# Where the first expert's weight splits, a route and six norms stand between the attention stage and the expert stages

## The chip, the cores and the metric

The kernel runs on one core of one Trainium2 chip. The metric is device time in microseconds, the median of the runs shown; one more execution was taken with the hardware profiler, and all rows of traces come from it. TensorE, VectorE, ScalarE, GpSimd (POOL) and the DMA queues each work through an instruction list of their own, in the order in which the program's scheduler put them, and wait for each other by semaphores. In the rows PE is TensorE's matmul, DVE is VectorE, ACT is ScalarE, SPq is the queue of SyncE, from which most transfers are issued.

## The reference, cut to what is computed

```python
kv  = einsum('bhsd,bhse->bhde', k, v)          # 4 x 8 heads, 576 rows, 64 columns
out = einsum('bhsd,bhde->bhse', q, kv)
x   = out / sqrt(mean(out*out, -1) + 1e-6) * g_norm      # -> 2304 rows of 512

# stage 1: one expert of 8 for each row
xn, en = x / (norm(x) + 1e-6), emb / (norm(emb) + 1e-6)
logits = xn @ en.T / tau
e      = argmax(logits);  gate = max(softmax(logits))
y      = gate * (relu(x @ w1[e]) @ w2[e])                # 512 -> 1024 -> 512

# stage 2: two experts of 8 for each row, noisy logits, weights from a softmax of the two
out    = sum over the two experts of weight * (relu(y @ w1b[e]) @ w2b[e])
```

All data is float32. The argmax of stage 1 needs only the direction of x, so the norm of a row enters the gate, not the choice of expert.

## The kernel before, in words

**Attention.** The 2304 rows lie in 18 tiles of 128 rows, in ten groups (`GROUPS`: two tiles each, but groups 4 and 9, which have one: tiles 8 and 17). For each group k of the loop at L592 the kernel multiplies q by the small matrices `kvm` (`out_mm`, L450; they also hold eight columns that give the logits), squares the results (`rms`, L465 on ScalarE, reduced at L466 on VectorE), takes 1/rms by Ln and Exp on ScalarE (L468, L469), and writes the scaled rows and logits (`out_fin`, L479 to L483, on VectorE). `q_turn` transposes q for the group two ahead (L440, copied on ScalarE at L442). `norms(k)` multiplies a tile by g (L490, VectorE) and sums its squares (L493, ScalarE) into `nx2`, which only the gate reads. It works in the buffers `xq` of the pool `at`; groups 0 to 4 (nine tiles) have their norms in the loop, groups 5 to 9 (nine tiles) behind it.

**Route of stage 1.** `route1(c0, c, psum)` takes the logits of c tiles: maximum, one-hot `hf`/`hb` on VectorE, ranks on TensorE (`ranks`, L200 to L203), slot numbers `si_all`, then c scatters on POOL (L211) that write the rows to `xs_dram`, sorted by expert. `FIRST` calls it in the loop for tiles 0 to 5, 6 to 10 and 11; it is called for tiles 12 to 17 behind the loop. Unit A is the first 256 rows of expert 0: its room is filled from tiles 0 to 11, so its rows are read back (`rows_of`, `xgA`) while attention still runs.

**Weights.** Each float32 weight is split into two fp32r parts, hi = round(w) on ScalarE (L256) and lo = w − hi on VectorE (L258), and a product is three matmuls (hi·hi, lo·hi, hi·lo). `w_load(g)` loads the g-th quarter of an expert's w1 and w2 into two staging buffers, `w_split(g, part)` splits one of them into a ring of four (`RING`; the first two, `PRE`, lie in `ring0`, the others in `ring1`, whose memory is that of the pool `at`). `W_AT` says behind which groups of attention g = 0 and 1 are split: 8 and 9. The names `st_377` and `st_381` are the staging buffers of g = 0 and 1.

**The seam.** Behind the loop stand, in the program: the route of the last six tiles (L622), the transposes of unit A's rows and their split into `xhA`/`xlA` (`x_parts`, L316 on ScalarE, L318 on VectorE; the transposes of the second half take the PSUM buffer `kvp`, which the route's ranks use too), four dummy products that keep TensorE at work (L635), and nine norms behind `xlA`. Then the pools `at` and `ap` close and the pools of the expert stages open on their memory: `mo` (SBUF) and `pp` (PSUM, tags `w` with three buffers and `acc` with five). `last_route` (L736) then counts rows (`slots_end`, L909, a small matmul that reads `cbb`), makes slots for padding rows, computes the gates (`gate1`) and writes them to memory.

**Expert stages.** `run` goes through units of rows and, for each, eight steps f of 128 of the 1024 inner columns: `mm1(u, f)` is 12 matmuls (L753), evicted as `hh` on ScalarE (L755) and `hl` on VectorE (L756); `mm2(u, f)` 12 more (L777) from `hh`, `hl`. So unit A is 8 × 24 = 192 matmuls of 256 columns. `hh`/`hl` have two buffers. Unit B is 128 more rows of expert 0; it needs its rows (`xgA` again) and, at its end, its gates (`ga1B`, gathered by POOL). Then come experts 1 to 7, and stage 2 in the same way. Between steps `weights_to` issues the next splits and loads. The zero-fill of `out` is transferred from a tile that a memset at L672 clears (tag `ot`, three buffers).

Of the kernel before, what the change touches and what calls it, by code (L numbers as in the profile page):

```python
# [8 lines left out]
F32 = mybir.dt.float32  # L9
# [7 lines left out]
P = 128  # L17
B, H, S, D = 4, 8, 576, 64
NT, DM, FF, E = B * S, H * D, 1024, 8
KD, KF = DM // P, FF // P  # L20
RB = S // D
# [11 lines left out]
XW = DM + E + 1  # L33
# [18 lines left out]
def attention_moe_moe_kernel(ctx: ExitStack, tc: tile.TileContext, q, k, v, g_norm, emb, tau, w1a, w2a,  # L52
# [293 lines left out]
    with tc.tile_pool(name="at", bufs=1) as at, \  # L346
# [9 lines left out]

        emb_t = at.tile([E, DM], F32, name="emb_t", tag="xq", bufs=2)
        G.dma_start(emb_t, emb)
# [125 lines left out]

        def norms(k):

            g, r, m = GROUPS[k]
            for c in range(g * RB + r, g * RB + r + m):
                xg = at.tile([P, H, D], F32, name="xq", bufs=2)
                V.tensor_tensor(xg, row_tile[c][:, 0:DM].rearrange("p (h d) -> p h d", d=D),  # L490
                                g_b.unsqueeze(1).to_broadcast([P, H, D]), op=OP.mult)
                xg = xg.rearrange("p h d -> p (h d)")
                A.activation(xg, xg, AF.Square, accum_out=nx2[:, c:c + 1])  # L493
# [98 lines left out]
        for k in range(last + 1):  # L592
            out_mm(k)
            if k == 1:
                for j in range(KD):
                    kv_part(1, j)
                kv_out(1)
                row_block(8, at.tile([P, 8, XW], F32, name="rows1", tag="ld", bufs=5), 4)
            if k in (2, 3):
                kv_m(k)  # L600
            rms(k)
            if k + 2 <= last:
                q_turn(k + 2)
            out_fin(k)
            if 1 <= k <= EARLY_N:
                norms(k - 1)
            if k in FIRST:
                with tc.high_priority():
                    for _ in route1(*FIRST[k], kvp):
                        pass  # L610
                    if k == 6:
                        more_room(cnt1, eoff1)
            if k == 6:
                masks(u1[0:1], u1[0].cnt)
                early.append(rows_of(u1[0]))
            if k in W_AT:
                g = W_AT.index(k)
                w_split(g, 0, V)
                w_split(g, 1, V)
        rooted = pin[0]  # L620
        pin[:] = None, None
        with tc.high_priority():  # L622
            for _ in route1(12, 6, kvp):
                pass
        u = u1[0]
        x = xs[u] = (c_tile([P, KD, A1], F32R, "xhA"), c_tile([P, KD, A1], F32R, "xlA"))
        for c in range(A1N):
            ps = ap.tile([P, 4, P], F32, name="kvp" if c else "qtp")
            for d in range(KD):
                turned = TE.transpose(ps[:, d, :], u.g[:, c, d * P:(d + 1) * P], ident)  # L630
            parted = x_parts(u, x, c, ps, rooted, add_counts.last)
        with tc.issue_after(turned.ins):
            ps = ap.tile([P, 2, 512], F32, name="op", bufs=3)
            for _ in range(4):
                TE.matmul(ps[:, 0, :], lhsT=ones, rhs=ones.unsqueeze(1).to_broadcast([P, 4, P]), start=True, stop=True)  # L635
        with tc.issue_after(parted[0].ins), tc.issue_after(parted[1].ins):
            for k in range(EARLY_N, last + 1):
                norms(k)
        G.dma_start(wgn[:, :, 0:E], w_gate.rearrange("(k p) e -> p k e", p=P))
# [6 lines left out]
        blank = spare[:, 0, :]  # L646
        w_load(PRE)
        w_load(PRE + 1)

# [86 lines left out]
    def last_route():  # L736
        with tc.high_priority():
            rest_of_firsts()
            gate1(0, TC)
            gates_out()  # L740

# [304 lines left out]
    def run(units, post):  # L1046
# [3 lines left out]
        for k, (u, f) in enumerate(steps):  # L1050
# [3 lines left out]
            if rows:  # L1054
# [4 lines left out]
                continue  # L1059
            if first:  # L1060
                if u.name == "A" and u.kind == 1:
                    last_route()
                mm1(u, f)
                first = False
# [257 lines left out]

W_AT = (8, 9)
EARLY_N = 5
WARM = 16
# [26 lines left out]
```

## Time and profile before

| | |
|---|---|
| median of 3 runs | 922.8 us (917.74 to 923.0) |
| profiled execution | 919.37 us, span 917.6 us |
| busy TensorE, VectorE, ScalarE, POOL | 90%, 52%, 35%, 32% of the span |
| mean granted TensorE clock | 0.955 of full speed |
| DMA | 133.7 MB, mean 146 GB/s |
| attention to the first product of unit A | 0 to 128.9 us |
| unit A | 128.9 to 154.2 us |

The profile is read by stretches: the busy shares over the whole span are a mean over stages with different limits. In rows of the timeline a line gives the start in us, how long, the engine, the line of the program, the output and input tile, shapes, and in brackets how long the engine stood idle before it and what released it. [...]

### The profile page before, as it was taken

How to read it: one execution, taken by the hardware profiler on the slowest of the kernel's cores; microseconds unless marked ns; L12 is line 12 of the kernel's file. 1: busy time of each engine (PE TensorE's matmuls, PEld its weight loads, DVE VectorE, ACT ScalarE, POOL GpSimd, SP SyncE). 2: the span in 40 equal slices, each digit the busy share in tenths (PEclk: the TensorE clock that was granted, in tenths of full speed). 3: DMA queues.
4: the chain of work that ended last, by engine and by line, in shares of the span. 5: the costliest groups of instructions: out<-in, count | busy, mean ns of one | idle time of the engine just before them, and what ended most of it. 6: DMA issues, size and time to landing. Idle time of an engine off the chain costs nothing. (4 is left out here: it accounts for less than half of the span.)

```text
span 917.6 us, 15847 instructions
## 1 busy us (share of the span) xinstructions
PE 827.8 (90%) x6190; PEld 753.9 (82%) x6190; DVE 481.6 (52%) x1370; ACT 323.7 (35%) x551; POOL 290.0 (32%) x299
## 2 busy tenths in 40 slices
PE   2778359999999999999969999999999999999993
PEld 1666249899999999998859998988989989899893
DVE  1248884688877967978435344333433333334211
ACT  0045452545435435434124233332323333332210
POOL 5002245428448457143352105023050140300303
PEclk7699669999999999999989999999999999999997
DMA  8961364837666676474266337355283371720404
GB/s 265 332 159 73 123 203 150 256 121 231 174 218 208 181 228 212 127 231 148 79 156 195 88 97 164 93 132 126 69 187 92 117 150 46 185 83 10 58 1 60
DMA packets 80480, 133.70 MB, mean 146 GB/s; under 512 B 10062, under 2 KB 42926, under 8 KB 79504
## 3 DMA queue, kind: packets, MB, share of 16 engines
q1 hardware_dynamic: 60448, 97.78, 35.1%
q0 software_dynamic: 17312, 28.96, 14.3%
q10 hardware_dynamic: 2640, 5.90, 2.0%
q8 instruction: 50, 0.82, 0.4%
q14 instruction: 30, 0.25, 0.1%
HBM read 97.80 MB, written 49.80 MB: 161 GB/s over the span
## 5 line engine op out<-in xcount | busy, mean ns | idle before, releaser
L753 PE MATMUL w<-xh,w1h 128*128 128x320 f32 (+3 forms) x736 | 236.1, 321 | 2.5 <-ACT xh L316 1.5
L753 PE MATMUL w<-xl,w1h 128*128 128x320 f32 (+3 forms) x736 | 229.6, 312 | 0.2 <-DVE xl L318 0.2
L753 PE MATMUL w<-xh,w1l 128*128 128x320 f32 (+3 forms) x736 | 229.7, 312 | 0.0
L755 ACT ACTIVATE hh<-w 128x320 fp32r<-128x320 f32 (+3 forms) x192 | 83.6, 436 | 229.9 <-PE w L753 207.6
L1011 POOL DMA_INDIRECT out_dram<-ot,to x35 | 55.3, 1581 | 295.9 <-DVE ot L1010 287.2
L756 DVE SCALAR_TENSOR_TENSOR hl<-w,hh 128x320 fp32r<-128x320 f32 (+3 forms) x192 | 92.8, 487 | 98.7 <-ACT hh L755 98.7
L753 PEld LDWEIGHTS w<-xh,w1h 128*128 128x128 f32 x736 | 139.3, 189 | 4.8 <-ACT xh L316 1.7
L753 PEld LDWEIGHTS w<-xl,w1h 128*128 128x128 f32 x736 | 139.7, 190 | 2.3 <-DVE xl L318 0.4
L753 PEld LDWEIGHTS w<-xh,w1l 128*128 128x128 f32 x736 | 139.2, 189 | 0.0
L779 PE MATMUL acc<-w2h,hl 128*128 128x512 f32 x320 | 126.8, 396 | 5.6 <-DVE hl L756 5.6
L779 PE MATMUL acc<-w2h,hh 128*128 128x512 f32 x320 | 127.4, 398 | 2.9 <-DVE ot L1010 2.8
L779 PE MATMUL acc<-w2l,hh 128*128 128x512 f32 x320 | 125.7, 393 | 0.0
L258 DVE TENSOR_TENSOR w2l<-st,w2h 128x1024 fp32r<-128x1024 f32 x64 | 79.8, 1246 | 79.0 <-ACT w2h L256 78.6
L258 DVE TENSOR_TENSOR w1l<-st,w1h 128x1024 fp32r<-128x1024 f32 x64 | 78.9, 1232 | 52.2 <-ACT w1h L256 51.9
L256 ACT ACTIVATE w2h<-st 128x1024 fp32r<-128x1024 f32 x64 | 67.7, 1058 | 90.9 <-PE acc L779 72.0
L256 ACT ACTIVATE w1h<-st 128x1024 fp32r<-128x1024 f32 x64 | 67.6, 1057 | 42.0 <-PE w L753 38.4
L777 PE MATMUL acc<-hl,w2h 128*128 128x336 f32 (+1 forms) x256 | 80.2, 314 | 0.4 <-DVE hl L756 0.4
L777 PE MATMUL acc<-hh,w2l 128*128 128x336 f32 (+1 forms) x256 | 79.9, 313 | 0.0
L777 PE MATMUL acc<-hh,w2h 128*128 128x336 f32 (+1 forms) x256 | 78.8, 316 | 0.0
L779 PEld LDWEIGHTS acc<-w2h,hl 128*128 128x128 f32 x320 | 60.3, 189 | 20.1 <-DVE hl L756 5.8
L779 PEld LDWEIGHTS acc<-w2h,hh 128*128 128x128 f32 x320 | 60.2, 188 | 16.1 <-DVE ot L1010 5.5
L779 PEld LDWEIGHTS acc<-w2l,hh 128*128 128x128 f32 x320 | 60.2, 188 | 10.7
(326 smaller groups left out, 1143.4 us busy)
## 6 DMA issues: line engine op xcount, KB each, us to landing
st<-in_moe_w_dram SPq DMA_DIRECT2D x128, 512.0 KB, 4.2
xg<-ys_dram SPq DMA_DIRECT2D x7, 1302.5 KB, 6.6
out_dram<-ot SPq DMA_DIRECT2D x7, 768.0 KB, 5.9
xg<-xs_dram SPq DMA_DIRECT2D x7, 683.8 KB, 5.5
q<-in_q_dram SPq DMA_DIRECT2D x3, 1152.0 KB, 19.7
k<-in_k_dram SPq DMA_DIRECT2D x2, 1152.0 KB, 20.5
k<-in_k_dram ACTq DMA_DIRECT2D x2, 1152.0 KB, 15.3
v<-in_v_dram SPq DMA_DIRECT2D x2, 1152.0 KB, 25.7
```

Source lines behind the costliest of these rows:

```text
L256: A.activation(hi, src, AF.Copy)
L258: eng.tensor_sub(lo, src, hi)
L753: last = TE.matmul(ps, lhsT=w[a][:, d, fo:fo + P], rhs=x[b][:, d, c0:c1], start=(d == 0 and i == 0), stop=(d == KD - 1 and i == 2))
L755: ra = A.activation(h[0][:, c0:c1], ps, AF.Relu)
L756: rv = V.scalar_tensor_tensor(h[1][:, c0:c1], ps, 0.0, h[0][:, c0:c1], op0=OP.max, op1=OP.subtract)
L777: TE.matmul(ac[j], lhsT=w_f[a][:, f % 2, j * P:(j + 1) * P], rhs=h_f[b][:, 0:u.m], start=st, stop=sp)
L779: TE.matmul(ac[j], lhsT=h_f[a][:, j * P:(j + 1) * P], rhs=w_f[b][:, f % 2, :], start=st, stop=sp)
L1011: i = G.indirect_dma_start(out=out, out_offset=bass.IndirectOffsetOnAxis(ap=u.to[:, t:t + 1], axis=0), in_=o, in_offset=None, bounds_check ...
```

## The change

Four things are edited.

1. `W_AT` becomes (1, 3): the weights g = 0 and 1 are split behind groups 1 and 3 of attention, and the loads of g = 2 and 3 are issued right behind each of these pairs of splits, where before they stood at the end of the seam.
2. The route of tiles 12 to 17 is no longer called at the seam. `last_route` now calls it, with a PSUM buffer of the expert stage, and `last_route` itself is called behind the first `mm1` of unit A, its instructions given to the scheduler as ones to be issued after that product.
3. `norms` takes a list of tiles, a pool, a name and a number of buffers. Groups 0 to 5 (tiles 0 to 10) and tile 11 have their norms in the loop, in `xq`; tiles 12 to 17 have theirs in `last_route`, between the count of rows and the gates, in the `ot` buffers of the pool `mo`.
4. Unit A's rows are split behind the last group's operations (`rooted` is now both pins: ScalarE's last Exp and VectorE's last logits), where VectorE's half stood behind the last route's counts.

```diff
-        def norms(k):
-            g, r, m = GROUPS[k]
-            for c in range(g * RB + r, g * RB + r + m):
-                xg = at.tile([P, H, D], F32, name="xq", bufs=2)
-                V.tensor_tensor(xg, row_tile[c][:, 0:DM].rearrange("p (h d) -> p h d", d=D),
+        def norms(cs, pool, nm, bufs):
+            for c in cs:
+                xg = pool.tile([P, XW], F32, name=nm, bufs=bufs)[:, 0:DM]
+                V.tensor_tensor(xg.rearrange("p (h d) -> p h d", d=D), row_tile[c][:, 0:DM].rearrange("p (h d) -> p h d", d=D),
                                 g_b.unsqueeze(1).to_broadcast([P, H, D]), op=OP.mult)
...
-            if 1 <= k <= EARLY_N:
-                norms(k - 1)
...
+            if 1 <= k <= 6:
+                norms(tiles(k - 1), at, "xq", 2)
+            elif k == 7:
+                norms((11,), at, "xq", 2)
             if k in W_AT:
                 g = W_AT.index(k)
                 w_split(g, 0, V)
                 w_split(g, 1, V)
-        rooted = pin[0]
+                w_load(PRE + g)
+        rooted = tuple(pin)
         pin[:] = None, None
-        with tc.high_priority():
-            for _ in route1(12, 6, kvp):
-                pass
...
-            parted = x_parts(u, x, c, ps, rooted, add_counts.last)
+            x_parts(u, x, c, ps, *rooted)
...
-        with tc.issue_after(parted[0].ins), tc.issue_after(parted[1].ins):
-            for k in range(EARLY_N, last + 1):
-                norms(k)
...
-        w_load(PRE)
-        w_load(PRE + 1)
...
     def last_route():
         with tc.high_priority():
+            for _ in route1(12, 6, misc):
+                pass
             rest_of_firsts()
-            gate1(0, TC)
-            gates_out()
+        norms(range(12, 18), mo, "ot", 3)
+        gate1(0, TC)
+        gates_out()
...
             if first:
+                m = mm1(u, f)
                 if u.name == "A" and u.kind == 1:
-                    last_route()
-                mm1(u, f)
+                    with tc.issue_after(m.ins):
+                        last_route()
                 first = False
...
-W_AT = (8, 9)
-EARLY_N = 5
+W_AT = (1, 3)
```

Three places show how the order of instructions moves. Line numbers of the changed kernel are up to six lower behind the edit (L753 becomes L749, L755 becomes L751, L777 becomes L773, L493 becomes L491, L909 becomes L905).

On ScalarE, in attention behind the Exp of group 3, before:

```order
L469 ACTIVATE ry<-rt 128x16
L442 COPY qT<-qtp 128x512
L468 ACTIVATE rt<-ss 128x8
L469 ACTIVATE ry<-rt 128x8
L442 COPY qT<-qtp 128x512
```

and now:

```order
L469 ACTIVATE ry<-rt 128x16
L256 ACTIVATE w1h<-st_381 128x1024
L256 ACTIVATE w2h<-st_382 128x1024
L468 ACTIVATE rt<-ss 128x8
L442 COPY qT<-qtp 128x512
L469 ACTIVATE ry<-rt 128x8
L442 COPY qT<-qtp 128x512
```

The pair of splits for g = 1 stands ahead of the copy of a transposed q tile (tile 11) and of group 4's Ln. The pair for g = 0 stands in the same way behind group 1's Exp.

On ScalarE at the seam, from the split of unit A's rows on, before (the staging buffers `st_1595` to `st_1600` hold g = 2 and 3):

```order
L316 ACTIVATE xhA<-qtp,g_99 128x4x128
L316 ACTIVATE xhA<-kvp,g_99 128x4x128
L493 ACTIVATE xq,nx_197<-xq 128x512 x9
L256 ACTIVATE w1h<-st_1595 128x1024
L176 ACTIVATE rtn<-nx_197 128x18
L256 ACTIVATE w2h<-st_1596 128x1024
L177 ACTIVATE ryn<-rtn 128x18
L256 ACTIVATE w1h<-st_1599 128x1024
L256 ACTIVATE w2h<-st_1600 128x1024
L755 ACTIVATE hh<-w 128x256 x8
```

and now (`st_788` to `st_1036` hold g = 2 and 3):

```order
L316 ACTIVATE xhA<-qtp,g_99 128x4x128
L316 ACTIVATE xhA<-kvp,g_99 128x4x128
L256 ACTIVATE w1h<-st_788 128x1024
L256 ACTIVATE w2h<-st_789 128x1024
L256 ACTIVATE w1h<-st_1035 128x1024
L491 ACTIVATE ot,nx_197<-ot 128x512
L751 ACTIVATE hh<-w 128x256
L491 ACTIVATE ot,nx_197<-ot 128x512 x3
L256 ACTIVATE w2h<-st_1036 128x1024
L491 ACTIVATE ot,nx_197<-ot 128x512 x2
L751 ACTIVATE hh<-w 128x256
```

Three splits and one norm stand ahead of the first eviction, five norms and a split between the first and the second.

On TensorE, between the dummy products and the first product of unit A, before:

```order
L635 LDWEIGHTS ones
L635 MATMUL op<-ones 128x512
L909 LDWEIGHTS ones
L909 MATMUL w<-cbb,ones 128x8
L753 MATMUL w<-xhA,w1h 128x256
```

and now, from the last of the first product's 12 matmuls (which follow the dummy products directly) to the ranks of the last six tiles:

```order
L749 MATMUL w<-xhA,w1l 128x256
L773 MATMUL acc<-hh,w2h 128x256 x4
L200 LDWEIGHTS tri
L200 MATMUL w<-hb,tri 128x48
L202 LDWEIGHTS ones
L202 MATMUL w<-hb,ones 128x40
```

Behind the ranks follow the other eight matmuls of the second product (from `hl`), then L905, then the first product of step 1. From unit B on, the order on TensorE, VectorE, ScalarE and the SP queue is the same before and now; on POOL the four subtractions `yl` of unit A now stand ahead of the gather of `ga1B`, where they stood behind three more gathers.

## Rows read from the trace of the kernel before

**Rows 1.** Page, part 1: busy us, share of the span, instructions of TensorE.
```profile
PE 827.8 (90%) x6190; PEld 753.9 (82%) x6190; DVE 481.6 (52%) x1370; ACT 323.7 (35%) x551; POOL 290.0 (32%) x299
```

**Rows 2.** Stretches: length, busy us of each engine, PEclk, DMA share, GB/s.
```profile
109.00:129.00 20.00, 3.54 (x19) 1.71 (x17) 16.87 (x43) 10.05 (x26) 7.24 (x7) 0.59 0.54 184
129.00:154.00 25.00, 24.59 (x192) 24.22 (x192) 15.78 (x54) 7.13 (x15) 10.32 (x15) 0.93 0.50 151
```

**Rows 3.** Waits, 100 to 129.2 us: who waited for whom, us, times, longest.
```profile
PE w L909 <- POOL xgA L140: 7.4, 1, 7.4
```

**Rows 4.** Timeline of TensorE, 108 to 155 us.
```profile
108.11 1.12 PE L630 MATMUL qtp<-ident,xgA 128*128 128x128 f32 x4 [2.79 <-DMA xgA<-xs_dram]
...
117.57 0.22 PE L200 MATMUL kvp<-hb,tri 128*128 128x48 bf16 x1 [8.34 <-DVE hb L527]
...
128.94 0.56 PE L753 MATMUL w<-xhA,w1h 128*128 128x256 f32 x1
...
131.43 0.41 PE L753 MATMUL w<-xhA,w1l 128*128 128x256 f32 x1
...
132.28 0.32 PE L753 MATMUL w<-xhA,w1h 128*128 128x256 f32 x1
...
154.17 0.60 PE L710 MATMUL w<-ident,xgA 128*128 128x128 f32 x4
```

**Rows 5.** Timeline of VectorE, 109 to 141 us.
```profile
109.97 1.21 DVE L258 TENSOR_TENSOR w1l<-st,w1h 128x1024 fp32r<-128x1024 f32 x1
...
112.24 0.16 DVE L470 TENSOR_TENSOR rt<-ry 128x8 f32<-128x8 f32 x1
...
113.64 0.25 DVE L483 TENSOR_REDUCE lg<-lw 128x8 f32<-128x64 f32 x1
...
120.58 0.75 DVE L318 SCALAR_TENSOR_TENSOR xlA<-kvp,g,xhA 128x512 fp32r<-128x512 f32 x1 [1.24 <-ACT xhA L316]
121.25 1.28 DVE L490 TENSOR_TENSOR xq<-rows,g_b 128x512 f32<-128x512 f32 x2
...
128.64 0.17 DVE L907 CAST cbb<-cnt 128x8 bf16<-128x8 f32 x1 [0.79 <-ACT xq L493]
...
140.37 0.48 DVE L672 MEMSET ot<- 128x512 f32 x1 [1.80 <-DMA out_dram<-ot]
```

**Rows 6.** Timeline of ScalarE, 108 to 170 us.
```profile
108.17 1.04 ACT L256 ACTIVATE w2h<-st 128x1024 fp32r<-128x1024 f32 x1
109.34 0.21 ACT L469 ACTIVATE ry<-rt 128x8 f32<-128x8 f32 x1
...
127.89 0.63 ACT L493 ACTIVATE xq<-xq 128x512 f32<-128x512 f32 x1
128.42 0.19 ACT L493 ACTIVATION_READ_ACCUMULATOR xq<-xq 128x1 f32 x1
...
132.71 0.36 ACT L755 ACTIVATE hh<-w 128x256 fp32r<-128x256 f32 x1
...
169.03 0.69 ACT L813 ACTIVATE yr<-acc,ga1B 128x512 f32<-128x512 f32 x1 [0.21 <-PE acc L807]
```

**Rows 7.** Two stretches of attention, and VectorE's timeline at 65.5 us.
```profile
60.00:62.00 2.00, 1.50 (x79) 1.36 (x74) 0.91 (x2) 1.33 (x4) 0.00 (x0) 0.83 0.06 22
76.00:96.00 20.00, 14.97 (x333) 11.72 (x324) 16.62 (x63) 11.63 (x31) 7.25 (x7) 1.00 0.22 83
...
65.50 0.42 DVE L403 COPY kvm<-op 128x256 f32<-128x256 f32 x1 [4.59 <-PE op L394]
```

**Rows 8.** SP queue's timeline; DMA issues, 30 to 140 us: KB, us to landing.
```profile
129.81 0.34 SPq L310 DMA_DIRECT2D xgA<-xs_dram  x1
...
out_dram<-ot SPq DMA_DIRECT2D x1, 512.0 KB, 6.7
```

**Rows 9.** Timeline of POOL, 126 to 166 us.
```profile
126.66 1.17 POOL L211 DMA_INDIRECT xs_dram<-xg,si_all  x1 [0.30 <-issue]
...
162.94 2.83 POOL L958 TENSOR_TENSOR yl<-yT,yh 128x256 fp32r<-128x256 f32 x4
```

More of the change, by code (lines that the diff above doesn't have):

```diff
@@ L355, in load @@
                               src[2 * g + i].rearrange("h (p r) d -> p h (r d)", r=RB))
-        emb_t = at.tile([E, DM], F32, name="emb_t", tag="xq", bufs=2)
+        emb_t = at.tile([E, XW], F32, name="emb_t", tag="xq", bufs=2)[:, 0:DM]
         G.dma_start(emb_t, emb)
@@ L483, in out_fin @@
             pin[1] = V.tensor_reduce(lg[:, c0:c0 + n, :], lw[:, 0:n].rearrange("p n h e -> p n e h"), axis=AX.X, op=OP.add)
-        def norms(k):
-            g, r, m = GROUPS[k]
-            for c in range(g * RB + r, g * RB + r + m):
-                xg = at.tile([P, H, D], F32, name="xq", bufs=2)
-                V.tensor_tensor(xg, row_tile[c][:, 0:DM].rearrange("p (h d) -> p h d", d=D),
+        def norms(cs, pool, nm, bufs):
+            for c in cs:
+                xg = pool.tile([P, XW], F32, name=nm, bufs=bufs)[:, 0:DM]
+                V.tensor_tensor(xg.rearrange("p (h d) -> p h d", d=D), row_tile[c][:, 0:DM].rearrange("p (h d) -> p h d", d=D),
                                 g_b.unsqueeze(1).to_broadcast([P, H, D]), op=OP.mult)
-                xg = xg.rearrange("p h d -> p (h d)")
                 A.activation(xg, xg, AF.Square, accum_out=nx2[:, c:c + 1])
```

## The prediction, made before the changed kernel ran

> **What bounds the kernel now.** The page gives TensorE 90% of the span [rows 1]; so I looked for the stretch where it isn't busy. From 109 to 129 us it is busy 3.54 us of 20 at a mean granted clock of 0.59; from 129 to 154 it is busy 24.59 of 25 [rows 2]. This kernel is bound by TensorE except ahead of its expert stages, above all at the seam between attention and experts, and a change of the seam is worth what it takes off the start of the first product. The waits of that seam name two: 8.3 us until the last six tiles' route has its one-hot `hb`, and 7.4 us before L909 [rows 3, 4]. The second is put down to the POOL memset of `xgA`, which follows the last scatter, but L909 also reads `cbb`, which VectorE wrote at 128.64 behind the last of nine norms on whose ScalarE half (128.42 + 0.19) VectorE's queue was waiting [rows 4 to 6]. The first product L753 could have begun when the second half of `xlA` was there, at 120.58 + 0.75 = 121.3 [rows 5], but TensorE's queue has L909 ahead of it, so it begins at 128.94 [rows 4].
>
> Going back: `xlA`'s second half waits for the route (its transposes use the PSUM buffer that the route's ranks of 117.57 held), the route for the last logits (113.64), and these for two weight splits (109.97 to 112.24) that stand in VectorE's queue between tile 16's and tile 17's work [rows 4, 5]. The data itself was there long before: the rows of unit A were transposed from 108.11 [rows 4].
>
> **The change, term by term.** Times below are on the clock of the profiled execution.
>
> *1. Start of the first product.* The four splits leave the end of attention. Between the logits of tiles 15 and 16, which end where the splits begin (109.97), and the rest of tile 17's chain (112.24) nothing then stands on VectorE, so its last logits end 2.27 us earlier: 113.64 + 0.25 − 2.27 = 111.6 [rows 5]. ScalarE had the factor for tile 17 at 109.34 + 0.21 [rows 6], so that is not later than its inputs. Then come the two L318 halves (0.75 each, starts about 0.7 apart) and a tenth for the signal: 113.2 without any delay of attention. The transposes (twice 1.12 us from 108.1 [rows 4]) and the four dummy products behind them, some two more, end before, so they don't decide.
>
> What attention pays: the second pair of splits (k = 3, two of 1.21 on VectorE, two of 1.04 on ScalarE [rows 5, 6]) and three norms more (tiles 9 to 11; 0.64 each on VectorE, 0.63 + 0.19 on ScalarE). The first pair (k = 1) is hidden: VectorE sits idle 4.59 us until the second half's k·v product is read at 65.50, and ScalarE waits longer [rows 5, 7]; its weights have landed by then, since the DMA engines are down to 6% from 60 to 62 [rows 7]. If that cover were gone, it would cost 2.4. On VectorE the rest is 2.4 + 3 × 0.64 = 4.3 us from 76 us on. Its idle time from 76 to 96 is 20 − 16.62 = 3.4 us [rows 7]. So the floor is 4.3 − 3.4 = 0.9 (every gap up to 96 filled) and the ceiling 4.3 + 2.1 = 6.4 (none filled, and ScalarE's pair, which goes in front of a `qT` copy, adds itself). I followed the new order by hand from 78 us on: the `kvT` copy moves ahead of a wait, the splits then end about where the reduction of tiles 9 and 10 began before, two norms fall into waits for ScalarE, and the route's short operations interleave. That lands near the floor; I take 1.0. First product: 114.2, that is 14.7 us earlier.
>
> *2. Unit A takes longer.* Before it takes 154.17 − 128.94 = 25.2 us from its first product to the transposes of unit B [rows 4]. Into this stretch now move the route of the last six tiles, their norms and the ranks on TensorE:
> - ranks and the end count on TensorE: seven small bf16 products, the first of 0.22 at 117.57 [rows 4], and L905, which like L909 is smaller still: an estimate of 0.6 for all.
> - ScalarE's queue: behind `xhA` stand three splits of 1.04 and one norm (0.82) before the first `hh`. They can start at about 112.6 and end at 116.5; the first product, at half clock (12 × 0.213 = 2.6; four starts in 132.28 − 131.43 [rows 4]), ends at 116.8. So `hh` waits for nothing but itself: 0.4 us during which TensorE has no other work, since only one product is ahead of it.
> - `hl` of f = 1, whose PSUM buffer f = 3 needs: on VectorE it stands behind `nx`, which waits for the last norm on ScalarE, and a split (1.2): ready at about 124.3, wanted at 123.7: 0.6.
> - the memset at L672 (now L665) waits for the zero-fill of `out`, as it did before at 140.37. The fill is now issued at about 126 and takes 6.7 [rows 5, 8], so the memset goes at 133, and `hl` of f = 5 and the last gate operations behind it; TensorE is there about 1.4 us earlier: 1.4. In the profile of before the same wait was covered.
> - behind the gate chain the last `w1l`, `w2l` which came after the gates before, too: 0.7 by the same walk, of which I take 0.4 to have been there before; 0.3.
> - [...] The new start is broken by the wait for `hh` and the ranks; I put ten more matmuls at half clock, 10 × 0.09 = 0.9.
>
> Sum 4.2. Floor: 0.6, the ranks alone. Ceiling: 6 × 0.82 + 6 × 0.64 = 8.8, if what the norms put on ScalarE and VectorE is paid in full.
>
> In the trace, queued work does hold back what stands behind it: the first `hh` (132.71) ran directly behind four splits although its product's last matmul, the twelfth, was out at 131.84, 0.9 us before [rows 4, 6]. [...]
>
> *3. Unit B and later.* From unit B on every queue has the same order as before, so a shift of unit A shifts the rest if its inputs are there. Rows of B: the route's slot numbers come at about 121 (before 119.2), six scatters of some 1.3 follow as before, when the last ended at 126.66 + 1.17, and the load (issued 2.0 us after that [rows 8, 9]) is in at about 135; B's transposes are due at 143.7. Gate of B: its gather now stands behind four `yl` subtractions (2.83 us [rows 9]). What holds POOL ahead of it is the load of expert 1's rows, by the same walk some 4 us earlier than before; with it the gather runs at about 153 and lands by 156, due at 169.03 − 10.5 = 158.5 [rows 6]. Weights g = 2, 3 are now loaded during attention, and those of g = 4, 5 are issued on SP behind splits that come earlier. Cost: nothing; the cover left is 8 us for the rows and 2 to 3 for the gate.
>
> **Sum.** −14.7 + 4.2 = −10.5. The profiled execution took 919.4 us (span 917.6), so I expect 908.9 in its terms; it lies 3.4 below the median of the runs shown (922.8; 917.7 to 923.0), from which it would be 912.3. I predict 912.
>
> **Rivals.**
> - *The seam becomes bound by ScalarE and VectorE* (ceiling of term 2): −14.7 + 8.8 = −5.9, 917. For it: VectorE is already busy 15.78 us of unit A's 25 [rows 2]. Against: ScalarE only 7.13. Chance 0.13.
> - *Attention pays in full* (ceiling of term 1): 113.2 + 6.4 = 119.6, −9.3 + 4.2 = −5.1, 918. For it: VectorE is 83% busy in 76 to 96, so it is nearly the bound there. Against: its 3.4 idle us in the same stretch [rows 7]. Chance 0.10.
> - *It does not arrive*: the gate of B or expert 1's rows come at their old times, plus the 2.83 of the `yl` row, and unit B gives back most: −2 or so, 921. Against: all that feeds them is issued earlier. Chance 0.08.
> - *Slower: the clock doesn't come back in unit A.* The products now come in pieces. If all 192 of unit A ran at 0.213, 177 more would pay 0.09: 15.9, of which 0.9 is counted: −10.5 + 15.0 = +4.5, 927. It decides from 127 such matmuls on (11.4 / 0.09). Against: 76 to 96 us shows clock 1.00 with TensorE busy 14.97 of 20 [rows 7], and the waits counted above are at most 1.4. [...] Chance 0.05.
> - *The forecast*, −8 to −13: 0.64.
>
> **How the numbers follow.** The best case is both floors: 128.94 − (113.2 + 0.9) − 0.6 = 14.2, from the profiled execution's 919.4 gives 905; the two priced rivals end at 918. With a microsecond for the spread of runs: 904 to 919, which leaves out the slower rival and most of the third. A change under 1% (9.2 us) can hardly be told from none here. A gain over 9.2 holds most of the forecast, since 4.2 lies between its bounds and a median of runs may fall on either side: 0.58. Slower by over 1%: part of the clock rival and what I don't see, 0.04. The rest, 0.38, is a gain too small to tell.
>
> **What would show it.** Right: the first L749 at 113.8 to 115; the last logits at 111.6 to 113; `hh` of f = 0 right behind it; unit B's transposes at 142 to 145.5; from there every stage earlier by the same amount, no new wait of unit B on a gather. Wrong: L749 after 118 (attention paid), TensorE waiting in unit A for `hh` or `hl` more than 5 us in sum (seam bound), pitch 0.213 still at 125 us (clock), or ScalarE idle before L809 for `ga1B` (gate).

## The result, and the profile after

The changed kernel takes **909.99 us** (median of 3 runs, 909.52 to 910.32), the kernel before 922.8: a ratio of 0.988, 95% interval 0.985 to 0.991. A second set of runs gave 912.36 against 921.63, ratio 0.990 (0.987 to 0.994). The profiled execution has a span of 908.6 us, 9.0 less than before. 912 was predicted.

The sum of the prediction can be laid beside the two traces by five distances on TensorE's and VectorE's timelines (us; "predicted" follows the prediction's terms, "again" is a second profile of the same changed kernel):

| stretch | before | predicted | after | again |
|---|---|---|---|---|
| start to the end of the last logits (L483) | 113.9 | 112.6 | 114.0 | 113.8 |
| from there to the first product (L753, now L749) | 15.05 | 1.6 | 1.82 | 1.94 |
| unit A: first product to unit B's transposes | 25.2 | 29.4 | 27.5 | 27.9 |
| unit B's transposes to expert 1's first product | 17.2 | 17.2 | 20.9 | 20.5 |
| from there to TensorE's last row | 732.2 | 732.2 | 729.9 | 731.4 |
| sum | 903.5 | 893.0 | 894.1 | 895.6 |

The sum is 1.1 us from the predicted one, but its terms are off by more and nearly cancel: +1.4 (attention ends later), +0.2, −1.9 (unit A is shorter), +3.7 (given back behind unit B, where nothing was expected), −2.3 (the rest). That the total came so close is therefore partly luck: the last two have no counterpart in the prediction.

Two of the four series in which the experiments ran (1 to 4, and 11) were slower for every kernel, the one before too (933.6 and 937.2 us), with stops of ScalarE of up to 7.3 us that its rows put down to "remote" and nothing in the kernel explains; so each kernel is compared with the kernel before of its own series and by the distances of this table.

TensorE's timeline after, which answers to [rows 4]:

```profile
112.09 1.11 PE L628 MATMUL qtp<-ident,xgA 128*128 128x128 f32 x4 [4.41 <-DMA xgA<-xs_dram]
...
113.85 1.91 PE L633 MATMUL op<-ones 128*128 128x512 bf16 x4
115.82 0.41 PE L749 MATMUL w<-xhA,w1h 128*128 128x256 f32 x1
116.07 0.28 PE L749 MATMUL w<-xlA,w1h 128*128 128x256 f32 x1
...
118.60 0.71 PE L773 MATMUL acc<-hh,w2h 128*128 128x256 f32 x4 [1.08 <-issue]
...
135.56 0.39 PE L773 MATMUL acc<-hl,w2h 128*128 128x256 f32 x1 [1.39 <-DVE hl L752]
...
143.32 0.60 PE L703 MATMUL w<-ident,xgA 128*128 128x128 f32 x4
...
154.34 0.50 PE L803 MATMUL acc<-w2h,xl 128*128 128x512 f32 x1 [1.31 <-DVE xl L657]
...
164.21 1.15 PE L749 MATMUL w<-xh,w1h 128*128 128x336 f32 x2 [3.63 <-DVE xl L318]
...
893.73 0.39 PE L775 MATMUL acc<-w2h,hl 128*128 128x512 f32 x1
```

The 7.4 us wait of [rows 3] is gone. The first product stands directly behind the four dummy products, and its second matmul follows at 116.07, then one every 0.118 us: the granted clock is 0.50 under the dummy products (113.85 to 115.76) and 1.00 from the second matmul on. Before, unit A's matmuls ran at 0.213 us each while 0.50 was granted (128.94 to 132.28) and at 0.118, or 0.124 with waits, at 1.00 (132.28 to 154.17); half and full clock below mean these two, told by the time of a matmul. In unit A two waits stand out, 1.08 ahead of the first `mm2` and 1.39 for `hl`. Behind unit B a third, 3.63 us for `xl`, opens ahead of expert 1. Before, that product and the last row stood here:

```profile
171.35 0.68 PE L753 MATMUL w<-xh,w1h 128*128 128x336 f32 x2 [1.49 <-ACT xh L316]
...
903.11 0.40 PE L779 MATMUL acc<-w2h,hl 128*128 128x512 f32 x1
```

The two stretches of [rows 2], now (length, busy time and instructions of PE, PEld, DVE, ACT, POOL, then PEclk, DMA share, GB/s):

```profile
109.00:129.00 20.00, 15.69 (x114) 13.77 (x114) 18.78 (x72) 11.65 (x29) 6.90 (x8) 0.83 0.31 94
129.00:154.00 25.00, 20.95 (x166) 19.51 (x164) 15.40 (x32) 7.27 (x13) 18.21 (x24) 1.00 0.61 208
```

TensorE is busy 15.69 of the 20 us in which it was busy 3.54. VectorE (answering to [rows 5]) shows where the waits come from:

```profile
113.75 0.25 DVE L483 TENSOR_REDUCE lg<-lw 128x8 f32<-128x64 f32 x1
...
114.81 0.75 DVE L318 SCALAR_TENSOR_TENSOR xlA<-kvp,g,xhA 128x512 fp32r<-128x512 f32 x1
...
133.15 0.48 DVE L665 MEMSET ot<- 128x512 f32 x1 [2.48 <-DMA out_dram<-ot]
...
150.01 3.67 DVE L258 TENSOR_TENSOR w1l<-st,w1h 128x1024 fp32r<-128x1024 f32 x1 [0.70 <-ACT w1h L256]
...
163.39 1.86 DVE L318 SCALAR_TENSOR_TENSOR xl<-w,g,xh 128x448 fp32r<-128x448 f32 x3
```

The last logits end at 113.75 + 0.25, `xlA` at 114.81 + 0.75 = 115.56, the dummy products at 113.85 + 1.91 = 115.76: the chain behind the logits and the dummy products both end within about a quarter of a microsecond of the first product. The memset at 133.15 is the one the prediction names. ScalarE (answering to [rows 6]) waits for the transposes of unit A's rows, has the first `hh` behind three splits and a norm, and later a long wait for weights:

```profile
113.24 0.69 ACT L316 ACTIVATE xhA<-qtp,g 128x512 fp32r<-128x512 f32 x1 [2.50 <-PE qtp L628]
...
114.68 1.05 ACT L256 ACTIVATE w1h<-st 128x1024 fp32r<-128x1024 f32 x1
...
118.14 0.36 ACT L751 ACTIVATE hh<-w 128x256 fp32r<-128x256 f32 x1
...
157.75 1.06 ACT L256 ACTIVATE w1h<-st 128x1024 fp32r<-128x1024 f32 x1 [4.86 <-DMA st<-in_moe_w_dram]
...
161.55 0.67 ACT L809 ACTIVATE yr<-acc,ga1B 128x512 f32<-128x512 f32 x1
```

What is transferred beside that load stands on POOL's timeline (the first scatters of tiles 0 to 5 and of tiles 6 to 10, then the zero-fill of `ys_dram`, 1.3 MB, and the `yl` subtractions of [rows 9]) and SP's:

```profile
83.28 1.08 POOL L211 DMA_INDIRECT xs_dram<-rows,si_all  x1 [16.42 <-DVE kvT L411]
...
98.84 0.97 POOL L211 DMA_INDIRECT xs_dram<-rows,si_all  x1 [7.52 <-DVE si_all L534]
...
148.81 0.95 POOL L690 DMA_DIRECT2D ys_dram<-xgA  x1
149.58 3.01 POOL L954 TENSOR_TENSOR yl<-yT,yh 128x256 fp32r<-128x256 f32 x4
```
```profile
149.34 11.12 SPq L243 DMA_DIRECT2D st<-in_moe_w_dram  x3
```

The fill is issued half a microsecond ahead of the weight loads. Before, they were issued 4.8 us apart, and ScalarE waited 0.43 us:

```profile
155.36 0.94 POOL L697 DMA_DIRECT2D ys_dram<-xgA  x1
```
```profile
160.17 7.08 SPq L243 DMA_DIRECT2D st<-in_moe_w_dram  x3
```
```profile
164.12 1.06 ACT L256 ACTIVATE w1h<-st 128x1024 fp32r<-128x1024 f32 x1 [0.43 <-DMA st<-in_moe_w_dram]
```

### The profile page after: what moved, and what is told of

The parts are those of the page before. It is cut to its first block, busy times and chain, and to the rows that moved or that the text cites. A ratio compares the mean times of both kernels' runs of the same rounds, so it can differ in the third digit from the quotient of the medians.

```text
span 908.6 us, 15846 instructions
## 1 busy us (share of the span) xinstructions
PE 829.2 (91%) x6190; PEld 754.8 (83%) x6190; DVE 481.8 (53%) x1370; ACT 323.6 (36%) x551; POOL 287.6 (32%) x299
## 5 line engine op out<-in xcount | busy, mean ns | idle before, releaser
L749 PE MATMUL w<-xh,w1h 128*128 128x320 f32 (+3 forms) x736 | 236.8, 322 | 3.6 <-DVE xl L318 3.6
L749 PE MATMUL w<-xl,w1h 128*128 128x320 f32 (+3 forms) x736 | 230.3, 313 | 0.1
L749 PE MATMUL w<-xh,w1l 128*128 128x320 f32 (+3 forms) x736 | 230.0, 313 | 0.0
L751 ACT ACTIVATE hh<-w 128x320 fp32r<-128x320 f32 (+3 forms) x192 | 83.6, 436 | 231.2 <-PE w L749 208.5
L749 PEld LDWEIGHTS w<-xh,w1h 128*128 128x128 f32 x736 | 139.7, 190 | 5.8 <-ACT xh L316 3.8
L749 PEld LDWEIGHTS w<-xl,w1h 128*128 128x128 f32 x736 | 140.1, 190 | 2.1 <-DVE xl L657 0.4
L749 PEld LDWEIGHTS w<-xh,w1l 128*128 128x128 f32 x736 | 139.7, 190 | 0.0
L258 DVE TENSOR_TENSOR w1l<-st,w1h 128x1024 fp32r<-128x1024 f32 x64 | 80.8, 1262 | 54.0 <-ACT w1h L256 53.9
L773 PE MATMUL acc<-hl,w2h 128*128 128x336 f32 (+1 forms) x256 | 79.3, 312 | 1.5 <-DVE hl L752 1.4
L773 PE MATMUL acc<-hh,w2l 128*128 128x336 f32 (+1 forms) x256 | 79.4, 312 | 0.0
L773 PE MATMUL acc<-hh,w2h 128*128 128x336 f32 (+1 forms) x256 | 77.8, 315 | 1.1 <-issue 1.1
```

The source lines that it names most:

```text
L258: eng.tensor_sub(lo, src, hi)
L749: last = TE.matmul(ps, lhsT=w[a][:, d, fo:fo + P], rhs=x[b][:, d, c0:c1], start=(d == 0 and i == 0), stop=(d == KD - 1 and i == 2))
L751: ra = A.activation(h[0][:, c0:c1], ps, AF.Relu)
L773: TE.matmul(ac[j], lhsT=w_f[a][:, f % 2, j * P:(j + 1) * P], rhs=h_f[b][:, 0:u.m], start=st, stop=sp)
```

## The experiments

**Theory.** The gain is the earlier first product less what unit A grows; it needs the splits and the route out of the seam together; and 3.7 us of it are given back because the zero-fill now meets the weight load. **Rivals.** The splits alone make it; the order alone makes it; the loss behind unit B is the slow split at 150.01 and not the fill.

### 1. The early splits alone

On the kernel before:

```diff
                 w_split(g, 1, V)
+                w_load(PRE + g)
...
-        w_load(PRE)
-        w_load(PRE + 1)
...
-W_AT = (8, 9)
+W_AT = (1, 3)
```

> The kernel before with one part of the change: the four splits of g = 0 and 1 at k = 1 and k = 3, the loads of g = 2 and 3 right behind them; route and norms stay ahead of the first product. Theory (most of the gain comes from taking the last six tiles' route out of the way of the first product): the seam only loses the two or four splits of 1.2 us that stand in VectorE's chain from the logits to L909, the scatters and nine norms stay; first product 2 to 5 us earlier than 128.94, less what the start of the run varies, total 1 to 4 us faster than before. Rival (the splits were the seam): first product before 118, gain of 8 us or more, and the moved route and norms would be worth nothing.

Measured: 932.17 against 933.62, ratio 0.9986 (0.996 to 1.0012). From the last tile's reduction to its logits 4.64 us instead of 6.89, from there to the first product 13.03 instead of 15.05; unit A 25.2. TensorE:

```profile
135.81 0.17 PE L908 MATMUL w<-cbb,ones 128*128 128x8 bf16 x1 [7.39 <-POOL xgA L140]
135.84 0.56 PE L752 MATMUL w<-xhA,w1h 128*128 128x256 f32 x1
```

The seam is 4.3 us shorter, of which the total shows 1.3, with an interval from 3.7 faster to 1.1 slower. The wait ahead of the count is the old one, 7.39. The splits alone aren't the gain.

### 2. The order alone

On the changed kernel, as all that follow:

```diff
-                w_load(PRE + g)
...
         blank = spare[:, 0, :]
+        w_load(PRE)
+        w_load(PRE + 1)
...
-W_AT = (1, 3)
+W_AT = (8, 9)
```

> The changed kernel with the four splits back at the end of attention and the loads of g = 2 and 3 behind them; first product ahead of the route, late norms as in the change. Theory: first product at 117 to 119 instead of 115.8, since the w1 split of g = 0 and its VectorE half stand between the last logits and xlA, and hh and hl of the first f stand behind more splits; 3 to 5 us slower than the changed kernel, 7 to 9 us faster than before; attention itself ends about 0.7 us earlier. Rival (early splits carry the gain): within 3 us of the kernel before.

Measured: 932.04, ratio 0.9972 (0.9946 to 0.9999): 2.6 us faster, not 7 to 9. The first product comes 4.08 us behind the last logits, about as expected, but unit A takes 32.4 us:

```profile
129.20 0.55 PE L750 MATMUL w<-xhA,w1h 128*128 128x256 f32 x1 [6.03 <-DVE fm L193]
129.55 0.41 PE L750 MATMUL w<-xlA,w1h 128*128 128x256 f32 x1
```

TensorE stood idle 6.03 us between the dummy products and the first product, and then ran 10.9 us at 0.213 a matmul. At 0.118 that is at most 10.9 × 0.095 / 0.213 = 4.9 us less (waits of 0.99 and 0.49 us lie in the stretch too), so most of the 4.9 us that unit A has over the changed kernel's 27.5. The parts give 1.3 and 2.6 us alone, and the whole gave 9 to 13, though in other series. The distances agree: from the last tile's reduction to unit B's transposes the parts are 4.3 and 3.8 us shorter than before, the whole 13.2 (12.7 in the second profile). The early splits also keep the first product close behind the dummy products (0.06 us in the changed kernel against 6.03 here), and it runs at 0.118 a matmul there against 0.213 here.

### 3. Without the dummy products

```diff
-        with tc.issue_after(turned.ins):
-            ps = ap.tile([P, 2, 512], F32, name="op", bufs=3)
-            for _ in range(4):
-                TE.matmul(ps[:, 0, :], lhsT=ones, rhs=ones.unsqueeze(1).to_broadcast([P, 4, P]), start=True, stop=True)
```

> The changed kernel without the four dummy products that stand between unit A's transposes and its first product (they compute nothing that is read). The changed kernel's first product ran at pitch 0.118 from its first rows, although the granted clock was low shortly before. Theory A (the dummies between transposes and product bring the clock back): without them the first 12 to 24 products run at 0.213, 1 to 2.5 us slower than the changed kernel, first product at the same 115.8. Theory B (the transposes alone do): same time within 0.5 us, pitch 0.118 again. Theory C (the dummies stand in the way): first product earlier, up to 0.3 us faster.

Measured: 928.98, ratio 0.9933 (0.990 to 0.9965). 2.47 us of idle time ahead of the first product, then 9.3 us at 0.213; unit A 31.0. It points to theory A, with a larger price in unit A than expected; since the changed kernel itself did not run beside it, experiment 10 repeats it next to the kernel it is to be compared with.

### 4 and 11. The zero-fill of `ys_dram` early

```diff
         blank = spare[:, 0, :]
+        i = G.dma_start(ys_dram[0:C2, :].rearrange("(p t) c -> p t c", t=N2),
+                        blank.unsqueeze(1).to_broadcast([P, N2, XW]))
+        tc.keep_in_program_order(i)
...
-    u1[0].hooks.setdefault(4, []).append(zero_rows)
```

> The changed kernel with the zero fill of ys_dram (1.3 MB) issued by POOL right behind the xgA memset at 114 us, where the DMA engines are idle, instead of at 148.8; everything else as in the change (the yl subtractions on POOL come out behind two more gathers). In the changed kernel 10.9 us gained at unit B's transposes are 6.2 at the first product of expert 1 (166 us): the weight load issued at 149.34, half a microsecond behind the fill, lands 8.4 us later (before: 160.17, 3.9 us), ScalarE waits 4.86 us for it, and xl of expert 1 stands behind those splits in both queues. Theory: the load lands at 153 to 154, ScalarE's wait of 4.86 shrinks below 2, TensorE's 3.63 us wait for xl of expert 1 goes, and 1.5 to 3 us of the span are won (906 to 908.5 us), if nothing later absorbs it. Rival 1 (the loss is the w1l split of 3.67 us beside yl on POOL, not the fill): unless yl has moved off it, no gain. Rival 2 (later slack absorbs it, as 2.5 us came back by 365 us in the changed kernel): the first product of expert 1 earlier, the span within 0.7 us.

Measured: 923.04 against 933.62, ratio 0.9862 (0.9794 to 0.9929). TensorE's wait ahead of expert 1 fell to 1.48 us and ScalarE's wait for weights is gone, but the stretch from unit B to expert 1 took 22.0 us, since one of the stops fell into it, with TensorE waiting 3.51 us for what it evicts:

```profile
163.53 0.60 ACT L794 ACTIVATE yr<-acc 128x512 f32<-128x512 f32 x1 [4.21 <-remote]
```

So this run couldn't tell, and the same kernel was run again later:

> The changed kernel with the ys_dram fill at 114 us and nothing else, as in the fourth experiment, where ScalarE's stops hid its effect. Theory (the fill at 148.8 is what holds back the weight load and unit B's gate): unit B's transposes to expert 1's first product 17.0 to 17.8 us instead of 20.5 to 20.9, unit A still 27.5 to 28.3 (its memset wait of 1.4 to 1.8 us stays, with no gap ahead of the first product); 3 to 4 us faster than the changed kernel, 906 to 909.5 us where the kernel before takes 921.5. Rival (it takes the fills of out from blank as well, as in the eighth): 20 us and more from B's transposes to expert 1.

Measured: 927.28 against 937.16, ratio 0.9893 (0.9865 to 0.9922). From unit B to expert 1 it is 18.15 us, and ScalarE's wait for weights is gone here too, so the mechanism holds. But unit A took 30.0, not 27.5 to 28.3: 0.68 us of idle time ahead of the first product, then 8.1 us at 0.213. The gain expected of the total isn't shown by this kernel.

### The changed kernel again

> The changed kernel unaltered, so that the following three stand beside it on the same chip. Theory (the gain is the seam's, and the seam is the same on any chip): from the last logits to the first product 1.6 to 2.2 us (before: 15.05), from the first product to unit B's transposes 27.3 to 29.5 us (27.5 in its first profile, 29.8 and 31.0 in two variants on another chip where the first 12 to 30 matmuls ran at 0.213), 0.985 to 0.991 of the kernel before. Rival (the first profile was lucky): a unit A of 30 us or more, ratio 0.990 to 0.995.

Measured: 912.36 against 921.63, ratio 0.9903. The distances are in the table; all as the theory has them. Experiments 5 to 7 ran beside it.

### 5. The `yl` subtractions behind the gathers

```diff
+        def low():
             for d in range(KD):
                 (G if late or d % 2 else V).tensor_sub(yl[:, d, 0:m], yT[:, d, 0:m], yh[:, d, 0:m])
+        if u is not u1[0]:
+            low()
...
         yield
+        if u is u1[0]:
+            low()
```

> The changed kernel with the four yl subtractions of unit A on POOL issued behind the gathers of unit B and expert 1, where they stood before the change; nothing else moves. In the changed kernel they run from 149.58 to 152.59 and the w1l split of 150.01 on VectorE beside them takes 3.67 us instead of 1.22, the xl halves of unit B's second product come behind it, TensorE waits 1.31 us at 154.34. Theory: the split is back at 1.2 to 1.3 us and the 1.31 us wait goes; the first product of expert 1 does not come earlier by more than 0.5 us, since its xl stands behind splits that wait for a weight load (4.86 us at 157.75), so the span is within 1 us of the changed kernel. Rival 1 of the earlier experiment (the loss behind unit B is this split): expert 1's first product 1.3 us or more earlier, span 1 to 2 us shorter.

Measured: 913.89, ratio 0.9912 (0.9886 to 0.9939). VectorE's split and ScalarE's wait for weights:

```profile
152.50 1.22 DVE L258 TENSOR_TENSOR w1l<-st,w1h 128x1024 fp32r<-128x1024 f32 x1 [0.70 <-ACT w1h L256]
```
```profile
163.48 1.06 ACT L256 ACTIVATE w1h<-st 128x1024 fp32r<-128x1024 f32 x1 [5.50 <-DMA st<-in_moe_w_dram]
```

The split is back at 1.22 us and TensorE's 1.31 us wait for L657 is gone, and nothing is won: expert 1 comes 21.9 us behind unit B. The rival falls. The slow split was real, but the wait for weights behind it covers it.

### 6. The fills of `out` from zeros that are there

```diff
-        z = mo.tile([P, XW], F32, name="ot", bufs=3)[:, 0:DM]
-        V.memset(z, 0.0)
+        z = blank[:, 0:DM]
```

> The changed kernel with the zero fills of out taken from the row of zeros that already lies in SBUF (blank) instead of from freshly cleared ot tiles: eight memsets of VectorE go, and with them the wait of the fourth (133.15, behind the 6.7 us fill issued at 126.29). Theory: hl of f = 5 is no longer late, TensorE's 1.39 us wait at 135.56 goes, unit A is 1.0 to 1.4 us shorter than in the changed kernel run beside it; of this 0.5 to 1.4 us stay in the span. Rival (the gate chain, not the memset, makes hl late): the wait stays above 0.8 us and unit A is as long as before.

Measured: 912.84, ratio 0.9897 (0.9848 to 0.9947). Unit A is 25.1 us (114.52 to 139.64), 2.4 to 2.8 shorter, twice the expected; the waits for `hl` and `w1l` are both gone. Then expert 1 waits 6.40 us, and ScalarE shows for what:

```profile
159.47 0.69 ACT L808 ACTIVATE yr<-acc,ga1B 128x512 f32<-128x512 f32 x1 [5.22 <-DMA ga1B<-gt_dram,ti1B]
```

That is unit B's gate, the wait of the third rival: its gather, issued on POOL at 152.42 behind the fill and `yl`, has landed by 159.4. So whatever unit A gains is lost again at the same place, once by the weights and once by the gate, both behind the 1.3 MB fill, the gate also behind `yl`.

### 7. Both fills, and unit A's parts not held back

The edits of 4 and 6, and:

```diff
-            x_parts(u, x, c, ps, *rooted)
+            x_parts(u, x, c, ps)
```

> The changed kernel with three things together: the zero fill of ys_dram issued at 114 us instead of 148.8 (as in an earlier experiment), the fills of out from blank, and xhA and xlA of unit A not held behind the last logits' factor and sum. Theory: the first product comes with its data, 114.6 to 115.1 on the clock of the first profile, 0.7 to 1.2 us earlier against xgA's transposes (3.7 us from the first transpose to the first product now, 2.6 to 3.1 then); unit A 1.0 to 1.4 us shorter; the 3.63 us wait of expert 1's first product below 2; in all 2.5 to 5 us faster than the changed kernel beside it. Rival (what comes early waits again at expert 1's weights or later): the first product and unit B's transposes 2 us earlier, the span within 1 us.

Measured: 908.57, ratio 0.9847 (0.9812 to 0.9883), 3.8 us less than the changed kernel beside it. By steps the expectation was half right:

```profile
112.53 1.11 PE L628 MATMUL qtp<-ident,xgA 128*128 128x128 f32 x4 [4.26 <-DMA xgA<-xs_dram]
...
117.09 0.55 PE L751 MATMUL w<-xhA,w1h 128*128 128x256 f32 x1 [0.88 <-DVE xg L481]
...
146.56 0.60 PE L705 MATMUL w<-ident,xgA 128*128 128x128 f32 x4
...
163.74 0.68 PE L751 MATMUL w<-xh,w1h 128*128 128x336 f32 x2 [1.49 <-ACT xh L316]
```

From unit B to expert 1 it is 17.2 us, as before the change. But the first product comes 4.56 us behind the first transpose instead of 3.73: VectorE's list now mixes `xlA` with tile 17's steps, and 0.88 us of idle time was followed by 11.8 us at 0.213; unit A took 29.5.

### 8. Both fills

The edits of 4 and 6 alone.

> The changed kernel with the zero fill of ys_dram issued at 114 us and the fills of out from blank; xhA and xlA stay behind the last logits. In the earlier runs the one brought the first product of expert 1 to 17.2 us behind unit B's transposes (20.5 to 22.1 in every kernel with the fill at 148.8, 17.2 before the change), the other unit A down to 25.1 us (27.5 to 28.3). Theory (two losses in a row, each hidden by the other when one alone is taken away): first product to unit B's transposes 25.0 to 25.6, from there to expert 1's first product 17.0 to 17.6, that product at 157 to 160 us; 4 to 6.5 us faster than the changed kernel, 904 to 908 us, ratio to the kernel before 0.980 to 0.985. Rival (the next stages wait for something else that keeps its old time): ratio 0.987 or more with expert 1's first product at 160 us or earlier.

Measured: **907.29** against 921.34, ratio 0.9849 (0.9816 to 0.9883).

```profile
116.50 0.37 PE L751 MATMUL w<-xhA,w1h 128*128 128x256 f32 x1
116.71 0.28 PE L751 MATMUL w<-xlA,w1h 128*128 128x256 f32 x1
...
141.61 0.60 PE L705 MATMUL w<-ident,xgA 128*128 128x128 f32 x4
...
158.83 0.68 PE L751 MATMUL w<-xh,w1h 128*128 128x336 f32 x2 [1.49 <-ACT xh L316]
```

Unit A 25.1, then 17.2. Full clock from the second matmul, whose row is 0.28 us long as in the changed kernel. The median of all weight loads' landing times around the stretch, of the changed kernel (146 to 158 us) and of this one (144 to 156 us; SP's issues, KB each, us to landing):

```profile
st<-in_moe_w_dram SPq DMA_DIRECT2D x2, 512.0 KB, 6.7
```
```profile
st<-in_moe_w_dram SPq DMA_DIRECT2D x5, 512.0 KB, 3.9
```

6.7 us beside the fill (5.8 for four loads in the changed kernel's second profile), 3.9 without. Two losses stood in a row here. What 6 alone takes out of unit A is lost again behind unit B; 11 alone shortens the stretch behind unit B by 2.4 to 2.7 us, but lost the clock in unit A. Together they bring 5 us (0.9849 against the changed kernel's 0.9903; the two intervals overlap a little), and by the distances 6.1 us from the first product to expert 1.

### 9. The first `hh` ahead of the splits

As 8, and:

```diff
-        pin[:] = (ra, rv) if u.kind == 1 and f == KF - 1 else (None, None)
+        if u is not u1[0] or f not in (1, 2):
+            pin[:] = (ra, rv) if u.kind == 1 and (f == KF - 1 or u is u1[0] and f == 0) else (None, None)
```

> As the kernel with early ys_dram fill and fills of out from blank, and besides the splits of g = 2 and 3 held on ScalarE and VectorE behind the first hh and hl. In the changed kernel three splits of g = 2 and 3 and a norm run on ScalarE from 114.7 to 118.1 and TensorE waits 0.6 to 1.2 us for the first hh. Theory (term of the first hh): only two norms stand ahead of it, the wait falls to 0.3 to 0.7 us and unit A is 0.3 to 0.9 us shorter than in that kernel; the splits are not needed before f = 4, so nothing is late for them; time 0 to 1 us less. Rival (the splits come back as waits at f = 4 or 6): unit A as long or longer, a wait on w1l or w2l in it.

Measured: **905.09**, ratio 0.9817 (0.9787 to 0.9847), the lowest of all, though its interval overlaps that of 8. TensorE's wait ahead of the first `mm2` is 0.73 us (1.21 in 8), unit A 24.6:

```profile
119.08 0.70 PE L776 MATMUL acc<-hh,w2h 128*128 128x256 f32 x4 [0.73 <-issue]
```

### 10. As 8, without the dummy products

> As the kernel with early ys_dram fill and fills of out from blank, without the four dummy products between unit A's transposes and its first product (they compute nothing that is read). Runs so far: no wait or one of 0.36 us ahead of the first product and pitch 0.118 from the start; a wait of 0.88 or more and pitch 0.213 for all of its 12 matmuls and more. Theory: TensorE now stands idle about 2 us ahead of the first product, which runs at 0.213; 12 to 30 matmuls at 0.09 more, so unit A is 1.1 to 2.7 us longer than with the dummies, and the time 1 to 2.7 us more. Rival (the clock is up again by itself after the transposes): pitch 0.118, same unit A within 0.4 us.

Measured: 908.18, ratio 0.9855 (0.9827 to 0.9882).

```profile
108.54 1.11 PE L628 MATMUL qtp<-ident,xgA 128*128 128x128 f32 x4 [3.48 <-DMA xgA<-xs_dram]
...
112.85 0.58 PE L747 MATMUL w<-xhA,w1h 128*128 128x256 f32 x1 [2.35 <-DVE xlA L318]
113.23 0.41 PE L747 MATMUL w<-xlA,w1h 128*128 128x256 f32 x1
...
139.91 0.60 PE L701 MATMUL w<-ident,xgA 128*128 128x128 f32 x4
```

Unit A 27.06, 1.95 more than in 8, as expected; 7.6 us at 0.213. Of the total 0.9 us show, less than the intervals can tell. Together with 2 and 3: behind 2.35, 6.03 and 2.47 us of idle time the new start ran at 0.213; in 8 and the changed kernel, where transposes, dummy products and the first product follow each other without a pause, at 0.118.

## Why the prediction was right, step by step

**Start of the first product: right in mechanism, 1.6 us late.** Predicted 114.2, measured 115.82 and 115.75. The 2.27 us of the two splits left tile 17's chain exactly as worked out: from its reduction to its logits 6.89 us before, 4.64 in every kernel with early splits but 7, and 6.91 in experiment 2. The rest, logits to product, was 1.8 to 1.9 for 1.6. The tenth in it for a signal was an estimate that no run tests by itself; in the profile after, `hl` ends at 135.08 + 0.42 and the matmul that waited for it starts 0.06 later, at 135.56. What was off is attention, 114.0 instead of 112.6. The splits of k = 3 and the norms, which the term was about, came near their price: from the read at 65.5 us [rows 7] to the last tile's reduction it is 41.5 us before and 41.2 to 42.8 in seven profiles of kernels with early splits (a mean 0.6 over it; 1.0 was taken). The other 1.8 of the mean lies ahead of that read: 65.5 before, 65.3 to 68.9 in these seven. The pair of k = 1 didn't stand in VectorE's way: in all seven VectorE still waits 0.7 to 4.9 us for TensorE's k·v product at that read. In the profile after, 1.0 of the 1.1 us is there at ScalarE's copy of the first half's product, ahead of any split (before, then after):

```profile
36.22 0.37 ACT L403 COPY kvm<-op 128x256 f32<-128x256 f32 x1 [21.78 <-DVE kvm L403]
```
```profile
37.23 0.37 ACT L403 COPY kvm<-op 128x256 f32<-128x256 f32 x1 [22.07 <-DVE kvm L403]
```

Why the first 65 us vary by up to 3.6 us stays open. Experiment 10 reached that read at 65.3, so early splits don't force it; but experiment 2, without them, reached it at 65.55, and of the profiles with them only that of 10 was earlier, so that they have no part in it isn't shown.

One sentence of this term was wrong: transposes and dummy products "don't decide". The rows of unit A landed 4 us later than before (112.09 for 108.11), because POOL's scatters of tiles 6 to 10 start at 98.84 instead of 95.20, and 2.7 of these 3.6 us are there at the scatters of tiles 0 to 5 (83.28 after). The rows of before:

```profile
80.60 1.08 POOL L211 DMA_INDIRECT xs_dram<-rows,si_all  x1 [14.86 <-DVE lw L479]
...
95.20 0.97 POOL L211 DMA_INDIRECT xs_dram<-rows,si_all  x1 [6.64 <-DVE si_all L536]
```

So it goes mostly with the late attention: in experiment 10, with the same norms in the loop and attention on time, the transposes begin at 108.54. The dummy products ended 0.06 us before the first product: the cover was gone. On ScalarE it already cost something: `xhA` waited for the transposes, so the three splits began at 114.68 and not at 112.6, and the first `hh` came at 118.14.

**Unit A: +2.3 and +2.7 instead of +4.2.** The waits came where they were put: the first `hh` 1.08 and, in the second profile, 0.58 (predicted 0.4), the memset 1.39 and 1.75 (1.4), the last `w1l` 0.60 (0.3); `hl` of f = 1 made none (0.6). The mis-sized term is the clock: ten more matmuls at half clock were charged at 0.09 each, 0.9. The 0.09 is 0.213 less 0.124: before, 15 of unit A's 192 matmuls had started at 0.213 by 132.28, and the other 177, which the slower rival counts too, took 21.9 us. The ten more no run shows: the new start ran at full clock after 0.25 us (1.4 in the second) against 3.5 us before, a gain of up to 1.5. That the first rival (ScalarE and VectorE bind the seam) isn't near shows in 9: with the norms still there, unit A takes 24.6 us, less than before the change.

**Unit B and later: "nothing" was the step that failed.** 3.7 and 3.4 us were given back between unit B and expert 1. The cover was counted by each input's own time, rows and gate, but not by what else the DMA engines carry then. Coming earlier brought the zero-fill and the weight load together (experiments 4 to 8). The gate's rival, 0.08, named the place and one of its two waits, which shows only in 6. Of this loss 2.3 (0.7 in the second profile) came back between expert 1 and the end; experiments 5 to 10 lie from 731.0 to 735.2 there, so this is within their spread and not explained further.

**The slower rival** didn't come in the changed kernel, and its size was far off in the others: half clock lasted up to 11.8 us where there was a pause (7), 4.4 us more in unit A than in 8 and not 15, and at most 2.1 us where there was none.

**The signs it named.** Of those for being right only unit B's transposes (143.3) came: the last logits and the first product are past theirs, `hh` waited, and the stages behind unit B don't keep the gain. None of those for being wrong came.

## What to carry to other kernels

When work is taken out of a seam, look at what will then be issued at the same moment: here a 1.3 MB fill nobody was waiting for met the next weight load and a gather, and moving it into a stretch where the DMA engines were idle (busy share 0.00 from 112 to 116 us) gave back what it took (17.2 us from unit B to expert 1 in 8, as before the change). One loss can hide what is won ahead of it: the 2.4 us of experiment 6 showed in the total only when the fill was moved too (8). Ahead of a stage's first product, keep TensorE busy without a pause until its inputs are there: with pauses of 0.68 to 0.95 us between filler and product, unit A took about 2 to 4 us longer here.

## What the hardware showed that was not expected

**The clock after a short pause.** Transposes and four dummy products ran ahead of the first product in all these kernels but 3 and 10. With no idle time or 0.36 us of it ahead of the product, the products reached 0.118 us within 0.2 to 2.1 us (six profiles). With 0.68, 0.88, 0.95, 2.35, 2.47 and 6.03 us (experiments 11, 7, 4, 10, 3 and 2) they ran at 0.213 for 8.1, 11.8, 7.5, 7.6, 9.3 and 10.9 us; in 7 the granted clock is 0.50 from 109 to 129 us. The length of the pause doesn't set the price here: the kernel before and experiment 1 stood idle for 7.4 us and then ran at 0.213 for only 3.5 and 5.2 us. There the first products followed each other without a wait; in the six others waits of 0.2 to 1.0 us for `hh`, `hb` or `cbb` fell between them. That the half clock lasts longer because of these waits is a reading of the rows, and no run tests it by itself.

**VectorE beside POOL.** The split of 150.01 took 3.67 us while POOL subtracted `yl` (149.58 to 152.59); in experiment 5, where they are apart, it took 1.22. In all fourteen profiles every split between 135 and 185 us that took more than 1.3 us ran beside `yl`: one more took 3.17 us (6), the others 1.3 to 1.9. The slow split cost nothing here, since it was hidden: without it, 5 was no faster (ratio 0.9912 against 0.9903).
